# The inverse of the FFT's B stage: six float32r matmuls replaced by plain float32 ones, issued sooner

## The chip, the cores and the metric

The kernel runs on one core of a Trainium2 chip. The time is device microseconds of one execution; the kernel before took 3709.85 us in the median of 3 runs (3709.05 to 3711.37). The profile is of one further execution.

## The reference

Three layers follow each other. The first is a global convolution by FFT over the sequence; the second a feed-forward layer whose activation g is 0 below -1, (h+1)²/4 between -1 and 1 and h above; the third sends each token to the one of eight experts with the largest gate logit.

```python
X = np.fft.rfft(x, axis=1)                        # x: 8 x 3072 x 256, float32
Y = X * (filt_r + 1j * filt_i)[None]
x = np.fft.irfft(Y, n=3072, axis=1).reshape(24576, 256)
x = g(x @ w_in) @ w_out                           # 256 -> 2048 -> 256
out[mask_e] = gate * (np.maximum(x[mask_e] @ w1[e], 0) @ w2[e])   # e = argmax(x @ w_gate), 8 experts, 1024
```

## The kernel before

The FFT of 3072 points is done as 128 x 24, in `fft_unit(u)` for each of the 8 sequences u. Stage A multiplies by a 128x128 table (`a_mm`, 12 half-groups) and stores the result in DRAM scratch. Stage B works on 16 groups g of two blocks each: `b_fwd` (line 459) multiplies by a forward table, `b_mul` and `b_add` (474, 484) multiply by the filter, and `b_inv` (500) multiplies by an inverse table; the result `z` goes back to scratch. `a_inv` (637) then undoes stage A directly into the inputs `xh`, `xl` of the feed-forward layer.

Unit 0 runs first, with plain float32 matmuls. In it the inverse adds two products, of `xq` and of `xs`, in PSUM. Units 1 to 7 run inside the feed-forward layer. They use float32r operands: each is split into a high part (the table's has its last 12 bits cleared) and the rest, and `mm` (356, its matmuls stand as line 361 in the trace) sums three products. For the inverse, ScalarE's `b_yh` (488, instruction at 491) makes the high part `yh` of `xq`, VectorE's `b_yl` (494, instruction at 497) the rest `yl`. The table's two parts come in one load `tt` on GpSimd's queue (`b_tab`, 434).

The feed-forward layer has 48 blocks of 512 tokens, 8 units n each. A unit has four steps: `l1(n, 0)`, `l1(n, 1)`, `l2(n-2, 0)`, `l2(n-2, 1)`, 12 matmuls each (lines 672 and 702). Between them VectorE clamps (679), ScalarE squares (680), VectorE takes a maximum (685), ScalarE rounds to float16 (`gh`, 688) and GpSimd subtracts for the rest (`gl`, 689). The hidden layer's PSUM tile `hps` has two buffers and is freed by line 685.

On TensorE, VectorE, ScalarE and GpSimd the order is the program's, written out by hand: `ev(s, f)` puts f behind step s, and `fire` calls it there. A step number is called a slot when TensorE gets FFT work there. Slots come from a planner (938 to 947): a heap of wishes in order of time, each with a `hold` for the two PSUM buffers `fps` that all FFT matmuls share, and a `bound` below which it may not be put. A group of stage B asks for its forward slot s at `h + b0 + bsp * g`; its table is loaded BT steps before, `b_hi` and `b_lo` (split of the input `a`) 9 and 8 steps before, VectorE's `b_mul` is at s + 2, GpSimd's at s + BX (3), `b_add` at s + BA (4), `b_yh` at s + BH (7 in unit 1, else 8), `b_yl` at s + BLO (9 or 10), and the inverse asks for s + BI (12 or 15). A forward slot's bound keeps it behind the release of buffers by earlier groups.

```python
            for i, (a, b) in enumerate(((ah, bh), (ah, bl), (al, bh))):
                PE.matmul(p, lhsT=a, rhs=b, start=i == 0, stop=i == 2)
```

VectorE and GpSimd also do the routing of each block: small instructions at lines 751 to 801, `hilo` (811) and four scatters by an indirect DMA (815).

Of the kernel before, what the change touches and what calls it, by code (L numbers as in the profile page):

```python
# [29 lines left out]
CVA, WI0 = 4, 8  # L30
AL, AX1, AX2 = 15, 9, 8
BL, BS1, BS2, BM, BV, BZ = 14, 9, 8, 2, 11, 2
BC = ((3, 4, 7, 9, 12, 7), (3, 4, 8, 10, 15, 10))
A1, A2 = (4, 3.5), (-58, 5.0)
B1, B2 = (60, 5.6), (20, 7.9)
ZL, ZB, AI, XL = 20, 8, (17, 12), 2
# [24 lines left out]
def _tables():  # L61
    s1, s2 = np.arange(S1), np.arange(S2)
    a = np.zeros((128, 128))
    ai = np.zeros((128, 128))
    for c in range(64):
        r, i = 2 * c, 2 * c + 1
        if c == 0:
            a[:, r], a[:, i] = 1.0, (-1.0) ** s1
            ai[r], ai[i] = 1.0 / NSEQ, (-1.0) ** s1 / NSEQ
        else:  # L70
            th = 2 * np.pi * ((s1 * c) % S1) / S1
            a[:, r], a[:, i] = np.cos(th), -np.sin(th)
            ai[r], ai[i] = 2 * np.cos(th) / NSEQ, -2 * np.sin(th) / NSEQ
    k2 = np.concatenate([np.arange(12), np.arange(23, 11, -1)])
    bf = np.zeros((NQ, 128, 128))
    bi = np.zeros((NQ, 128, 96))
    fr = np.full((NQ, 128), -1)
    fi = np.full((NQ, 128), -1)
    j12 = np.arange(12)
    for q in range(NQ):  # L80
        for kb in range(2):
            c = 2 * q + kb
            xr = slice(48 * kb, 48 * kb + 24)
            xi = slice(48 * kb + 24, 48 * kb + 48)
            o_r, o_i = 24 * kb, 64 + 24 * kb
            if c > 0:
                th = 2 * np.pi * ((s2[:, None] * (c + 128 * k2[None, :])) % NSEQ) / NSEQ
                co, si = np.cos(th), np.sin(th)
                low = np.arange(24) < 12
                s = np.where(low, -1.0, 1.0)  # L90
                r, i = slice(o_r, o_r + 24), slice(o_i, o_i + 24)
                bf[q, xr, r], bf[q, xi, r] = co, si
                bf[q, xr, i], bf[q, xi, i] = -si * s, co * s
                bi[q, r, xr], bi[q, i, xr] = co.T, (-si * s).T
                bi[q, r, xi], bi[q, i, xi] = si.T, (co * s).T
                f = np.where(low, c + 128 * k2, NSEQ - (c + 128 * k2))
                fr[q, r] = fr[q, i] = fi[q, r] = fi[q, i] = f
            else:
                t0 = 2 * np.pi * ((s2[:, None] * 128 * j12) % NSEQ) / NSEQ
                t1 = 2 * np.pi * ((s2[:, None] * (64 + 128 * j12)) % NSEQ) / NSEQ  # L100
                alt = (-1.0) ** s2
                bf[q, xr, 0:12] = np.cos(t0)
                bf[q, xr, 65:76] = np.sin(t0)[:, 1:]
                bf[q, xr, 64] = alt
                bf[q, xi, 12:24] = np.cos(t1)
                bf[q, xi, 76:88] = np.sin(t1)
                bi[q, 0:12, xr] = (np.where(j12 == 0, 1.0, 2.0) * np.cos(t0)).T
                bi[q, 65:76, xr] = (2 * np.sin(t0)[:, 1:]).T
                bi[q, 64, xr] = alt
                bi[q, 12:24, xi] = (2 * np.cos(t1)).T  # L110
                bi[q, 76:88, xi] = (2 * np.sin(t1)).T
                f = np.concatenate([128 * j12, 64 + 128 * j12])
                fr[q, 0:24] = fi[q, 0:24] = fr[q, 64:88] = fi[q, 64:88] = f
                fr[q, 64] = NSEQ // 2
                fi[q, 0] = fi[q, 64] = -1
    cst = np.zeros((128, C_W))
    cst[:, C_A:C_A + 128] = a
    cst[:, C_AI:C_AI + 128] = ai
    cst[:, C_ID:C_ID + 128] = np.eye(128)
    cst[:, C_TRI:C_TRI + 128] = np.triu(np.ones((128, 128)), 1)  # L120
    cst[:, C_ONE:C_ONE + 128] = 1.0
    cst[:, C_TOK:C_TOK + S2] = 24 * np.arange(128)[:, None] + s2
    cst[:, C_EC:C_EC + E] = np.arange(E) - E
    cst[:, C_ECAP:C_ECAP + E] = np.arange(E) * CAP
    cst[:, C_T:C_T + NT] = np.arange(NT)
    cst[:, C_P] = np.arange(128)
    tab = np.concatenate([bf, bi], axis=2).astype(np.float32)
    hi = (tab.view(np.int32) & ~0xFFF).view(np.float32)
    return cst.astype(np.float32), np.stack([tab, hi, tab - hi]), fr, fi


@with_exitstack
def tile_kernel(ctx, tc, x, w_in, w_out, w_gate, w1, w2, cst, tab, fil, out):
    nc = tc.nc
    V, A, PE, G, SP = nc.vector, nc.scalar, nc.tensor, nc.gpsimd, nc.sync

# [34 lines left out]
    if True:  # L171
# [207 lines left out]
        def fft_unit(u):  # L379
# [44 lines left out]
            def b_load(g):  # L424
                if u:
                    tt = None
                else:
                    tt = alt(u, g, [128, 1, 2, 224], "tt", (qp, "tt"), (fp, "wst"), (qp, "tt"), (fp, "wst"), (fp, "wst"))
                    SP.dma_start(tt, tab[g, :, 0:1])
                tf = more(g, 2, 1, [128, 2, 2 * D], F32, "tf") if u else alt(u, g, [128, 2, 2 * D], "tf", (qp, "tf"), (fp, "xh"), (fp, "xl"))  # L430
                pin(u, g, *((tf, fil[g]) if u or g == 0 else (tf[0:64], fil[g, 0:64])))
                st["b", g] = (tt, tf)

            def b_tab(g):
                tt = more(g, 2, 2, [128, 2, 2, 224], F32R, "tt")
                G.dma_start(tt, tab[g, :, 1:3])
                st["b", g] = (tt,) + st["b", g][1:]

            def b_dup(g):
# [19 lines left out]
            def b_fwd(g):  # L459
                tt, _, t, ag, al = (st["b", g] + (None, None))[0:5]  # L460
                p = ups(u)
                for i in range(2):
                    pi = p[:, i * D:(i + 1) * D]
                    if u:
                        mm(pi, tt[0:96, 0, i, 0:128], tt[0:96, 1, i, 0:128], ag[:, i, :], al[:, i, :])
                    else:
                        mm(pi, tt[0:96, 0, i, 0:128], None, t[:, i, :], None)
                xs = alt(u, g, [128, 2, D], "xs", (qp, "xs"), (fp, "gh"))
                pv = p.rearrange("p (b d) -> p b d", b=2)
                A.activation(xs[0:64], pv[64:128], AF.Copy)  # L470
                A.activation(xs[64:128], pv[0:64], AF.Copy, scale=-1.0)
                st["p", g] = (pv, xs)
# [12 lines left out]
                xq, xs = st["q", g]  # L485
                G.tensor_tensor(xq, xq, xs, op=ALU.add)

            def b_yh(g):
                xq, _ = st["q", g]
                yh = more(g, 2, 1, [128, 2, D], F32R, "yh")  # L490
                A.activation(yh, xq, AF.Copy)
                st["q", g] = (xq, yh)

            def b_yl(g):
                xq, yh = st["q", g]
                yl = more(g, 2, 1, [128, 2, D], F32R, "yl")
                V.tensor_tensor(yl, xq, yh.bitcast(F32), op=ALU.subtract)
                st["q", g] = (yh, yl)

            def b_inv(g):  # L500
                tt = st.pop(("b", g))[0]
                yh, yl = st.pop(("q", g))
                p = ups(u)
                for i in range(2):
                    pi = p[0:96, i * D:(i + 1) * D]
                    if u:
                        mm(pi, tt[:, 0, i, 128:224], tt[:, 1, i, 128:224], yh[:, i], yl[:, i])
                    else:
                        PE.matmul(pi, lhsT=tt[:, 0, i, 128:224], rhs=yh[:, i], start=True, stop=False)
                        PE.matmul(pi, lhsT=tt[:, 0, i, 128:224], rhs=yl[:, i], start=False, stop=True)  # L510
                z = qx[0].tile([96, 2, D], F32, tag="z", name="z", bufs=2) if u else \
                    alt(u, g, [96, 2, D], "z", (qp, "ao"), (qp, "xi"), (qp, "xg"), (qp, "xr"))
                A.activation(z.rearrange("p q d -> p (q d)"), p[0:96], AF.Copy)
# [39 lines left out]
            h = 192 * (u - 1)  # L553
            a0, asp = A1 if u == 1 else A2
            b0, bsp = B1 if u == 1 else B2
            BX, BA, BH, BLO, BI, BT = BC[u > 1]
            ax1, ax2 = (AX1 - 3, AX2 - 3) if u == 1 else (AX1, AX2)

            sa, sb, si = [], [], []
# [6 lines left out]
            def b_bound(g):  # L566
                if len(sb) < g or len(sa) < 2 * NA:
                    return None
                if g == 0:
                    return sa[-1] + BL + 3  # L570
                if g < 3:
                    return sb[0] + 1 + max(BS1, BLO - BM) if g == 2 else 0
                if len(si) < g - 3:
                    return None
                return max(si[g - 4] + BT + 1 if g > 3 else 0, sb[g - 2] + 1 + max(BS1, BLO - BM), sb[g - 3] + 1 + BI + BV - BH)

            def a_slot(s, g, i):
                sa.append(s)
# [6 lines left out]
            def b_slot(s, g):  # L585
# [7 lines left out]
                ev(s + BM, lambda: b_mul(g, 0))  # L593
                ev(s + BX, lambda: b_mul(g, 1))
                ev(s + BA, lambda: b_add(g))
                ev(s + BH, lambda: b_yh(g))
                ev(s + BLO, lambda: b_yl(g))
                slot(s + BI, lambda s: i_slot(s, g), 4 - (u == 1))

            def i_slot(s, g):  # L600
# [581 lines left out]


def _arrays(inputs):
    cst, tab, ir, ii = _tables()

    def lay(a, idx):
        a = np.concatenate([a, np.zeros((1, D), a.dtype)])
# [2 lines left out]
    def pairs(a):  # L1191
# [8 lines left out]
        "w1": a['moe2_w1'],  # L1200
        "w2": a['moe2_w2'],
        "cst": cst,
        "tab": np.ascontiguousarray(tab.reshape(3, NQ // 2, 2, 128, 224).transpose(1, 3, 0, 2, 4)),
        "fil": pairs(np.concatenate([lay(a['filt_r'], ir), lay(a['filt_i'], ii)], axis=2)),
    }

# [13 lines left out]
```

## Time and profile before

| | |
|---|---|
| runs of the kernel before, median (range) | 3709.85 us (3709.05 to 3711.37) |
| the profiled execution | 3699.91 us |
| its span | 3698.1 us |
| TensorE matmuls (PE) busy | 3512.2 us, 95% |
| VectorE (DVE) busy | 2496.0 us, 67% |
| GpSimd (POOL) busy | 1945.8 us, 53% |
| ScalarE (ACT) busy | 1823.4 us, 49% |
| mean granted TensorE clock | 0.983 |

Times are microseconds from the start of the span. A row of a view names a source line (L485 is line 485), an engine, an operation, the tile written and the tiles read, and how often it ran (x112). Matmuls are pipelined: one's duration is longer than the distance to the next one's start, so distances between starts are what a matmul costs TensorE.

### The profile page before, as it was taken

How to read it: one execution, taken by the hardware profiler on the slowest of the kernel's cores; microseconds unless marked ns; L12 is line 12 of the kernel's file. 1: busy time of each engine (PE TensorE's matmuls, PEld its weight loads, DVE VectorE, ACT ScalarE, POOL GpSimd, SP SyncE). 2: the span in 40 equal slices, each digit the busy share in tenths (PEclk: the TensorE clock that was granted, in tenths of full speed). 3: DMA queues.
4: the chain of work that ended last, by engine and by line, in shares of the span. 5: the costliest groups of instructions: out<-in, count | busy, mean ns of one | idle time of the engine just before them, and what ended most of it. 6: DMA issues, size and time to landing. Idle time of an engine off the chain costs nothing. (4 is left out here: it accounts for less than half of the span.)

```text
span 3698.1 us, 75021 instructions
## 1 busy us (share of the span) xinstructions
PE 3512.2 (95%) x30690; PEld 3068.5 (83%) x30690; DVE 2496.0 (67%) x3494; ACT 1823.4 (49%) x2544; POOL 1945.8 (53%) x1428
## 2 busy tenths in 40 slices
PE   6799999999899999999999999999999999999998
PEld 4688888788788878888888888888888888888887
DVE  6678889979888987987888799867632222222222
ACT  4556655655666665666656565554422222222221
POOL 1367666657656765776666576444332222222222
PEclk8899999999999999999999999999999999999999
DMA  9445445434434443444444353101232222222221
GB/s 290 124 132 163 152 142 151 125 124 138 126 122 138 138 129 125 139 128 132 138 127 137 109 145 114 46 24 62 55 84 51 52 52 52 49 53 52 52 52 50
DMA packets 323820, 395.32 MB, mean 107 GB/s; under 512 B 163791, under 2 KB 250063, under 8 KB 322960
## 3 DMA queue, kind: packets, MB, share of 16 engines
q1 hardware_dynamic: 274848, 279.90, 26.6%
q0 software_dynamic: 48624, 110.58, 9.7%
q8 instruction: 243, 3.98, 0.5%
q14 instruction: 105, 0.86, 0.1%
HBM read 439.70 MB, written 120.49 MB: 151 GB/s over the span
## 5 line engine op out<-in xcount | busy, mean ns | idle before, releaser
L689 POOL TENSOR_TENSOR gl<-cl,gh 128x1024 f16<-128x1024 f32 x384 | 821.5, 2139 | 812.6 <-ACT gh L688 527.9
L672 PE MATMUL hps<-xh,wih 128*128 128x256 f16 x3072 | 844.9, 275 | 36.2 <-DVE cl L685 35.7
L672 PE MATMUL hps<-xl,wih 128*128 128x256 f16 x3072 | 842.5, 274 | 1.7 <-DVE xl L646 1.7
L672 PE MATMUL hps<-xh,wil 128*128 128x256 f16 x3072 | 842.2, 274 | 0.0
L702 PE MATMUL yps<-woh,gh 128*128 128x264 f16 x3072 | 721.1, 278 | 13.7 <-ACT ysb L715 13.5
L702 PE MATMUL yps<-wol,gh 128*128 128x264 f16 x3072 | 719.5, 277 | 0.0
L1080 DVE SCALAR_TENSOR_TENSOR hl<-mh,hh 128x1024 f16<-128x1024 f32 x194 | 237.7, 1225 | 686.9 <-ACT hh L1079 678.5
L679 DVE TENSOR_SCALAR cl<-hps,sq 128x1024 f32<-128x1024 f32 x384 | 514.5, 1340 | 273.3 <-PE hps L672 223.5
L680 ACT ACTIVATE cl<-cl,sq 128x1024 f32<-128x1024 f32 x384 | 476.0, 1240 | 448.2 <-DVE cl L679 353.6
L672 PEld LDWEIGHTS <-wih 128*128 128x128 f16 x6144 | 588.0, 98 | 129.8 <-DVE cl L685 37.9
L702 PEld LDWEIGHTS <-gh 128*128 128x128 f16 x6144 | 589.6, 98 | 121.3 <-issue 29.0
L688 ACT ACTIVATE gh<-cl 128x1024 f16<-128x1024 f32 x384 | 406.0, 1057 | 528.7 <-DVE cl L685 527.7
L685 DVE SCALAR_TENSOR_TENSOR cl<-hps,sq,cl 128x1024 f32<-128x1024 f32 x384 | 490.2, 1277 | 101.5 <-ACT cl L680 94.1
L1071 PE MATMUL mh<-xt,wslot 128*128 128x256 f16 x4656 | 540.0, 273 | 0.0
L1079 ACT ACTIVATE hh<-mh 128x1024 f16<-128x1024 f32 x194 | 198.6, 1024 | 620.1 <-PE mh L1071 429.7
L1071 PEld LDWEIGHTS <-wslot 128*128 128x128 f16 x4656 | 455.6, 98 | 52.7
L702 PE MATMUL yps<-woh,gl 128*128 128x264 f16 x3072 | 414.7, 279 | 6.6 <-POOL gl L689 6.6
L1094 PE MATMUL my<-wslot,hh 128*128 128x256 f16 x3104 | 370.8, 273 | 2.8 <-ACT o L1108 2.8
L702 PEld LDWEIGHTS <-gl 128*128 128x128 f16 x3072 | 303.4, 99 | 55.2 <-POOL gl L689 7.2
L1111 POOL DMA_INDIRECT out_dram<-o,me x194 | 191.5, 987 | 281.6 <-issue 200.2
L1094 PEld LDWEIGHTS <-hh 128*128 128x128 f16 x3104 | 303.6, 98 | 38.6 <-issue 3.4
L672 PEld LDWEIGHTS <-wil 128*128 128x128 f16 x3072 | 302.4, 98 | 38.9 <-issue 2.1
(204 smaller groups left out, 4707.5 us busy)
## 6 DMA issues: line engine op xcount, KB each, us to landing
tf<-in_fil_dram SPq DMA_DIRECT2D x113, 512.0 KB
tt<-in_tab_dram POOLq DMA_DIRECT2D x112, 448.0 KB
wst<-in_w_dram SPq DMA_DIRECT2D x128, 256.0 KB
xi<-in_x_dram SPq DMA_DIRECT2D x48, 512.0 KB
scr<-ao SPq DMA_DIRECT2D x48, 512.0 KB
a<-scr SPq DMA_DIRECT2D x128, 192.0 KB
scr<-z SPq DMA_DIRECT2D x128, 192.0 KB
zt<-scr SPq DMA_DIRECT2D x48, 512.0 KB
```

The costliest lines, as they stand in the source:

```text
L672: PE.matmul(p[:, i, :], lhsT=w[:, kt, f * 128:(f + 1) * 128], rhs=xx[:, kt, s], start=a == 0, stop=a == 5)
L679: V.tensor_scalar(cl, p, q[:, 5:6], q[:, 3:4], op0=ALU.max, op1=ALU.min)
L680: A.activation(cl, cl, AF.Square, bias=q[:, 11:12], scale=q[:, 4:5])
L685: V.scalar_tensor_tensor(cl, p, q[:, 7:8], cl, op0=ALU.mult, op1=ALU.max)
L688: A.activation(gh, cl, AF.Copy)
L689: G.tensor_tensor(gl, cl, gh, op=ALU.subtract)
L702: PE.matmul(yps[j][:, 0:WO], lhsT=gg[:, i, j * 128:(j + 1) * 128], rhs=w[:, f, :], start=f == 0 and first, stop=f == NF - 1 and gg is gl)
L1071: PE.matmul(p[:, i, :], lhsT=w[:, wo + kt * FE + f * 128:wo + kt * FE + f * 128 + 128], rhs=xt_[:, xo + kt, :], start=a == 0, stop=a == 5)
L1079: A.activation(hh, p, AF.Relu)
L1080: V.scalar_tensor_tensor(hl, p, 0.0, hh, op0=ALU.max, op1=ALU.subtract)
L1094: PE.matmul(yq[t][j][:, 0:D], lhsT=hx[:, i, j * 128:(j + 1) * 128], rhs=w[:, wo + f * D:wo + (f + 1) * D], start=f == 0 and first, stop=f ...
L1111: G.indirect_dma_start(out=out, out_offset=IOA(ap=me.bitcast(I32)[:, tk, 1:2], axis=0), in_=o, in_offset=None, bounds_check=NTOK - 1, oob_ ...
```

## The change

In units 1 to 7 the inverse multiplies `xq` itself, by the undivided table, with a plain float32 matmul; `b_yh` and `b_yl` are gone. The inverse half of the table is loaded by a second DMA on GpSimd's queue into a tile `ti`, undivided; the forward half keeps its two parts (512 values a partition, then 192, where there were 896). The inverse asks for s + 9 in unit 1 and s + 10 in the others. The bound of a forward slot is written anew: a group's `xq` must not be written before the inverse two groups earlier has read it. Unit 0 keeps its instructions; its table is an array of its own.

```diff
-BC = ((3, 4, 7, 9, 12, 7), (3, 4, 8, 10, 15, 10))
+BC = ((3, 4, 9, 7), (3, 4, 10, 10))
...
-                    SP.dma_start(tt, tab[g, :, 0:1])
+                    SP.dma_start(tt[:, 0], tab[g])
...
             def b_tab(g):
-                tt = more(g, 2, 2, [128, 2, 2, 224], F32R, "tt")
-                G.dma_start(tt, tab[g, :, 1:3])
+                tt = more(g, 2, 2, [128, 512], F32R, "tt"), more(g, 2, 2, [128, 192], F32, "ti")
+                G.dma_start(tt[0], tab2[g, :, 0:512])
+                G.dma_start(tt[1], tab2[g, :, 512:704])
...
-                        mm(pi, tt[0:96, 0, i, 0:128], tt[0:96, 1, i, 0:128], ag[:, i, :], al[:, i, :])
+                        mm(pi, *(tt[0][0:96, o + 128 * i:o + 128 * i + 128] for o in (0, 256)), ag[:, i, :], al[:, i, :])
...
-            def b_yh(g):
-                xq, _ = st["q", g]
-                yh = more(g, 2, 1, [128, 2, D], F32R, "yh")
-                A.activation(yh, xq, AF.Copy)
-                st["q", g] = (xq, yh)
-
-            def b_yl(g):
-                xq, yh = st["q", g]
-                yl = more(g, 2, 1, [128, 2, D], F32R, "yl")
-                V.tensor_tensor(yl, xq, yh.bitcast(F32), op=ALU.subtract)
-                st["q", g] = (yh, yl)
-
             def b_inv(g):
...
                     if u:
-                        mm(pi, tt[:, 0, i, 128:224], tt[:, 1, i, 128:224], yh[:, i], yl[:, i])
+                        mm(pi, tt[1][:, 96 * i:96 * i + 96], None, xq[:, i], None)
...
-            BX, BA, BH, BLO, BI, BT = BC[u > 1]
+            BX, BA, BI, BT = BC[u > 1]
...
-                if g < 3:
-                    return sb[0] + 1 + max(BS1, BLO - BM) if g == 2 else 0
-                if len(si) < g - 3:
+                if len(si) < g - 1:
                     return None
-                return max(si[g - 4] + BT + 1 if g > 3 else 0, sb[g - 2] + 1 + max(BS1, BLO - BM), sb[g - 3] + 1 + BI + BV - BH)
+                return max(si[g - 4] + BT + 1 if g > 3 else 0, sb[g - 2] + 1 + BS1 if g > 1 else 0, si[g - 2] + 1 - BM if g > 1 else 0)
...
-                ev(s + BH, lambda: b_yh(g))
-                ev(s + BLO, lambda: b_yl(g))
```

## Rows read from the trace of the kernel before

**Rows 1.** Busy time (instructions) by stretch: start:end, length, PE, PEld, DVE, ACT, POOL, PEclk, DMA, GB/s.

```profile
135.00:2330.00 2195.00, 2077.95 (x18074) 1805.95 (x18073) 1848.52 (x2449) 1349.14 (x1945) 1465.76 (x1013) 0.99 0.44 133
2330.00:3698.10 1368.10, 1342.09 (x12236) 1196.57 (x12234) 555.45 (x857) 409.34 (x501) 452.57 (x386) 0.99 0.21 52
```

**Rows 2.** Waits of PE, 135 to 2330 us: total us, times, longest us.

```profile
PE hps L672 <- DVE cl L685: 33.2, 22, 3.6
PE fps L361 <- DVE xl L646: 21.8, 11, 4.2
PE yps L702 <- ACT ysb L715: 13.5, 12, 2.1
PE fps L361 <- ACT ao L420: 11.3, 3, 4.1
PE fps L361 <- DVE xq L479: 9.6, 8, 1.7
```

**Rows 3.** Groups by line: shapes, xcount | busy us, mean ns | idle before, by releaser.

```profile
L361 PE MATMUL fps<-yh,tt 128*96 128x256 f32 x448 | 106.9, 301 | 14.7 <-DVE xq L479 8.7 <-DVE xl L646 5.5
...
L361 PE MATMUL fps<-yl,tt 128*96 128x256 f32 x224 | 63.5, 283 | 3.6 <-DVE oh L756 3.6
```

**Rows 4.** Timeline of PE around one inverse: start us, us, instruction.

```profile
1170.18 0.27 PE L672 MATMUL hps<-xh,wil 128*128 128x256 f16 x1
...
1170.99 0.28 PE L672 MATMUL hps<-xh,wih 128*128 128x256 f16 x1
```

**Rows 5.** Timeline of PE in unit 0: two products of an inverse, and the next one.

```profile
68.44 0.59 PE L509 MATMUL hps<-xq,tt 128*96 128x256 f32 x2
...
69.30 0.59 PE L509 MATMUL hps<-xq,tt 128*96 128x256 f32 x2
```

**Rows 6.** Timeline of PE around float32 matmuls of `a_inv`.

```profile
1077.35 0.28 PE L702 MATMUL yps<-wol,gh 128*128 128x264 f16 x1
1077.46 1.05 PE L644 MATMUL fps<-c,zt 128*128 128x128 f32 x8
1078.35 0.28 PE L702 MATMUL yps<-woh,gh 128*128 128x264 f16 x1
```

**Rows 7.** Groups by line, 135 to 2330 us: the two splits of `xq`.

```profile
L497 DVE TENSOR_TENSOR yl<-xq,yh 128x512 fp32r<-128x512 f32 x112 | 163.3, 1458 | 10.3 <-ACT yh L491 10.1
...
L491 ACT ACTIVATE yh<-xq 128x512 fp32r<-128x512 f32 x112 | 69.5, 620 | 27.1 <-POOL xq L486 26.9
```

**Rows 8.** Timeline, 1170 to 1176 us, with [idle before <-releaser].

```profile
1170.51 0.63 ACT L491 ACTIVATE yh<-xq 128x512 fp32r<-128x512 f32 x1 [1.19 <-POOL xq L486]
...
1173.95 0.27 PE L702 MATMUL yps<-woh,gh 128*128 128x264 f16 x1 [1.47 <-ACT ysb L715]
```

**Rows 9.** Groups by line of POOL, 135 to 2330 us.

```profile
L689 POOL TENSOR_TENSOR gl<-cl,gh 128x1024 f16<-128x1024 f32 x326 | 697.9, 2141 | 657.3 <-ACT gh L688 456.8 <-issue 189.5 <-PE fps L361 7.3
...
L436 POOL DMA_DIRECT2D tt<-in_tab_dram x112 | 66.4, 593 | 0.1
```

**Rows 10.** Timeline: a forward, its addition, and the step behind the new slot.

```profile
1152.70 0.36 PE L361 MATMUL fps<-ag,tt 96*128 96x256 f32 x1
...
1167.63 0.28 PE L702 MATMUL yps<-woh,gh 128*128 128x264 f16 x1
...
1169.19 1.28 POOL L486 TENSOR_TENSOR xq<-xq,xs 128x512 f32<-128x512 f32 x1
```

**Rows 11.** Instructions on tile `xq`: ns min/median/max, first and last start us.

```profile
L486 POOL TENSOR_TENSOR xq<-xq,xs x112: 1259/1284/1770, 246.3 to 2314.0; 128x512 f32<-128x512 f32 x112
```

**Rows 12.** Timeline of DVE and POOL, 1156 to 1162 us.

```profile
1156.35 0.68 DVE L479 TENSOR_TENSOR xq<-fps,tf 128x512 f32<-128x512 f32 x1
1156.95 4.72 DVE L811 SCALAR_TENSOR_TENSOR row<-ysb,sm,row 128x256 f16<-128x256 f32 x1
...
1156.58 1.05 POOL L815 DMA_INDIRECT rows<-row,posi  x1 [0.17 <-DVE cl L679]
...
1160.07 1.31 POOL L486 TENSOR_TENSOR xq<-xq,xs 128x512 f32<-128x512 f32 x1
```

More of the change, by code (lines that the diff above doesn't have):

```diff
@@ L128, in _tables, with tile_kernel @@
     hi = (tab.view(np.int32) & ~0xFFF).view(np.float32)
-    return cst.astype(np.float32), np.stack([tab, hi, tab - hi]), fr, fi
+    tab2 = np.stack([hi[:, :, 0:128], (tab - hi)[:, :, 0:128]])
+    return cst.astype(np.float32), tab, tab2, fr, fi
 @with_exitstack
-def tile_kernel(ctx, tc, x, w_in, w_out, w_gate, w1, w2, cst, tab, fil, out):
+def tile_kernel(ctx, tc, x, w_in, w_out, w_gate, w1, w2, cst, tab, tab2, fil, out):
     nc = tc.nc
@@ L486, in b_add @@
                 G.tensor_tensor(xq, xq, xs, op=ALU.add)
-            def b_yh(g):
-                xq, _ = st["q", g]
-                yh = more(g, 2, 1, [128, 2, D], F32R, "yh")
-                A.activation(yh, xq, AF.Copy)
-                st["q", g] = (xq, yh)
-            def b_yl(g):
-                xq, yh = st["q", g]
-                yl = more(g, 2, 1, [128, 2, D], F32R, "yl")
-                V.tensor_tensor(yl, xq, yh.bitcast(F32), op=ALU.subtract)
-                st["q", g] = (yh, yl)
             def b_inv(g):
                 tt = st.pop(("b", g))[0]
-                yh, yl = st.pop(("q", g))
+                xq, xs = st.pop(("q", g))
                 p = ups(u)
@@ L506, in b_inv @@
                     if u:
-                        mm(pi, tt[:, 0, i, 128:224], tt[:, 1, i, 128:224], yh[:, i], yl[:, i])
+                        mm(pi, tt[1][:, 96 * i:96 * i + 96], None, xq[:, i], None)
                     else:
-                        PE.matmul(pi, lhsT=tt[:, 0, i, 128:224], rhs=yh[:, i], start=True, stop=False)
-                        PE.matmul(pi, lhsT=tt[:, 0, i, 128:224], rhs=yl[:, i], start=False, stop=True)
+                        PE.matmul(pi, lhsT=tt[:, 0, i, 128:224], rhs=xq[:, i], start=True, stop=False)
+                        PE.matmul(pi, lhsT=tt[:, 0, i, 128:224], rhs=xs[:, i], start=False, stop=True)
                 z = qx[0].tile([96, 2, D], F32, tag="z", name="z", bufs=2) if u else \
@@ L1184, in _arrays @@
 def _arrays(inputs):
-    cst, tab, ir, ii = _tables()
+    cst, tab, tab2, ir, ii = _tables()
     def lay(a, idx):
@@ L1202, in _arrays @@
         "cst": cst,
-        "tab": np.ascontiguousarray(tab.reshape(3, NQ // 2, 2, 128, 224).transpose(1, 3, 0, 2, 4)),
+        "tab": pairs(tab),
+        "tab2": np.concatenate([tab2.reshape(2, NQ // 2, 2, 128, 128).transpose(1, 3, 0, 2, 4).reshape(NQ // 2, 128, 512),
+                                pairs(tab[:, :, 128:224]).reshape(NQ // 2, 128, 192)], axis=2),
         "fil": pairs(np.concatenate([lay(a['filt_r'], ir), lay(a['filt_i'], ii)], axis=2)),
```

## The prediction, made before the change was run

> **What bounds the kernel now.** I read the stretches first. Of the span of 3698.1 us, 2195 us (135 to 2330 us) are those in which FFT units 1 to 7 run between the steps of the first feed-forward layer, and only there does the change touch anything but a table's layout. In it TensorE is busy 2078 us, VectorE 1849, GpSimd 1466, ScalarE 1349, and the DMA engines 44% of the time; behind 2330 us nothing of the change is left [rows 1]. So TensorE bounds: 2195 - 2078 = 117 us are all that it idles. The second view is who ends that idling. The five longest entries are 33.2 us for `cl` (the half-layer's PSUM tile, freed by VectorE's line 685), 21.8 and 9.6 us for PSUM banks that VectorE frees (lines 646 and 479), 13.5 us for ScalarE's `ysb` and 11.3 us for its `ao`: 89.4 us together, 64.6 of them VectorE's [rows 2]. The reader is to see two prices from this. An instruction added to TensorE costs its whole duration, 112 times. One taken from VectorE or ScalarE is worth only what it shortens of those 117 us.
>
> **The change, part by part.** The sum is made against the profiled execution (3699.91 us), which is 9.94 us under the median of 3709.85; I carry the difference over to the median.
>
> *The inverse on TensorE.* Today a group's inverse is six float32r matmuls of 128x256 (three products, two halves): 448 + 224 instructions over 112 groups [rows 3]. At an undisturbed place the last layer matmul before it starts at 1170.18 and the first one behind it at 1170.99 us; layer matmuls follow each other after 0.11 us, so the inverse costs 0.81 - 0.11 = 0.70 us [rows 4]. The plain form is already here: unit 0 multiplies exactly this shape in float32, and each such matmul is issued as two instructions. Four of them, which is what a group will have, take from 68.44 to 69.30 us, 0.86 us [rows 5]. The other neighbour is the float32 matmul between layer matmuls, eight of 128 columns, as many columns as four of 256: 1078.35 - 1077.35 - 0.11 = 0.89 us [rows 6]. I take 0.86, the same shape: 112 x (0.86 - 0.70) = **+18 us**, all on the path; upper end 112 x 0.19 = 21, and nothing in the rows allows a gain.
> The Trainium skill (FP8 and Floating Point Precision, TensorE Precision Notes) says that a true float32 multiplication is four passes through the array where the reduced one is one, which speaks against the change. By it alone eight passes would replace six, so the 0.70 us would become 0.93, the term 26 us, and the sum -4 instead of -12; no row supports the larger figure, and the measured 0.86 decides.
>
> *What leaves VectorE and ScalarE.* The subtraction `yl` is 163.3 us of VectorE in 112 instructions, 1458 ns in the mean, and the copy `yh` 69.5 us of ScalarE [rows 7]. That is 9% of VectorE's work in the stretch. What of it TensorE sees I take entry by entry from [rows 2].
> For `ysb`: ScalarE runs in order, and at 1170.51 us `yh` has just waited 1.19 us for GpSimd's addition and takes 0.63; the `ysb` behind it then comes late and TensorE waits 1.47 us for it [rows 8]. Without `yh` both go; ten of 13.5 us, since not each of the twelve waits has this cause. For `cl`: one `yl` of 1.46 us ahead of line 685 is as long as one wait in the mean (33.2/22 = 1.5), so between nothing and 33.2 goes; I take 20, because VectorE's queue is often still full of other work. For the banks (21.8 + 9.6) I take a third, 10; for `ao`, whose copy is late for other reasons, nothing. Together **-40 us**; ends: -20 (`ysb` and half of `cl`'s 20) and -67 (`ysb`, `cl`, `xq` whole, half of `xl`).
>
> *The inverse moved sooner.* It is asked for 10 steps behind the forward transform instead of 15 (units 2 to 7), 9 instead of 12 in unit 1. Working the planner's heap through with both sets of constants, I find 10 to 16 steps instead of 15 to 20 in the later units. With it move its ScalarE copy `z`, VectorE's maximum two steps on, and the store on SP's queue, which passes loads of `x`, the filter and the scratch: nothing, the DMA engines being 44% busy [rows 1]; without that cover, the loads behind it would be late by one 192 KB store. The planner also moves forward slots and the routing by up to four steps, which decides where GpSimd's work bunches.
> What the inverse must now wait for is GpSimd's addition directly. A step is 2195/326/4 = 1.68 us, by the 326 `gl` of the stretch [rows 9], ten steps 16.8. In the worked example the forward matmul starts at 1152.70; its addition starts at 1169.19 and ends, after 1.28 us, at 1170.47; yet the step behind which TensorE will now want it is over at 1167.63: 2.84 us late [rows 10]. The same comparison for all 112 additions (246.3 to 2314.0 us, [rows 11]) against their new slots finds 26 late, by 44 us in all. That is the upper end, nothing the lower. Most of the lateness comes from queues that get shorter: in the example VectorE's line 811 lasts 4.72 us while GpSimd runs from 1156.58 through the addition that ends at 1161.38, and it holds `cl`, `gh` and so GpSimd's next work [rows 12]. In units 3 to 7 the forward ahead of it moves four steps off this bunch. I take **+10 us**. Queued behind a waiting inverse is the whole of TensorE, which is why this counts in full.
>
> *The table.* One load becomes two on GpSimd's queue, each with an issue of 0.59 us: +66 us of GpSimd over 112 groups [rows 9], which idles 2195 - 1466 = 729 us. I count nothing; without that cover each addition is 0.6 us later, and that lies inside the 44 us. Fewer bytes go; unit 0's load keeps its bytes.
> *The added wait.* `xq` is now read by TensorE until the inverse, so VectorE's product two groups on must wait for that inverse, and behind it line 679 or 685. The new bound in the planner keeps it at least a step behind; in the example VectorE comes to its product at 1156.35, 3.65 us after the forward's 1152.70 [rows 10, 12]. Nothing.
>
> **Sum:** 18 + 10 - 40 = -12 us: 3688 for the profiled execution, **3698** for the median.
>
> **The rivals.** A difference of 0.2% (7.4 us) is about what a measurement of this kernel can tell from none.
> (a) *Slower: TensorE waits for the addition.* Place: the inverse slot, ten steps behind the forward. For it: the 44 us above, and GpSimd gets 66 us more work. Against: 26 of 112 only, and shorter queues ahead. It decides once the addition ends over 16.8 us behind its forward in about a quarter of the groups, as today. Price 34 of the 44, with 30 of the 40 regained: 18 + 34 - 30 = +22, 3732 us.
> (b) *No difference: the blocking stays.* VectorE's two-input instructions stand still while GpSimd runs back to back; the 4.72 us above belong to a 128x256 instruction of line 811, not to `yl` [rows 12]. If `yl` goes, the next such instruction stands in its place and only its own work is saved. The relief is then 28: 18 + 10 - 28 = 0, 3710 us. The Trainium skill (SBUF — State Buffer, SBUF: two separate sides) has this as an exclusive lock on a shared port pair, under which the loser blocks fully; the trace agrees, with 4.72 us.
> (c) *A larger gain:* relief of 67 and no late addition: 18 - 67 = -49, 3661 us.
> (d) *The change doesn't do what it says:* the slots stay where they were because bounds push them. The planner's arithmetic speaks against; with the inverse late, 18 - 20 = -2, 3708 us.
>
> **How the numbers follow.** Forecast 50%, (a) 23%, (b) 18%, (c) 7%, (d) 2%. Of the forecast's half I put 41 points beyond 0.2% and 9 within, as its terms can miss by 5 either way and more; of (b) 12 points lie within and 3 on each side; (d) within. Faster: 41 + 3 + 7 = 51%; same: 9 + 12 + 2 = 23%; slower: 23 + 3 = 26%. The range reaches from (c) to (a), 3661 to 3732; what is left out are the outer halves of both, under 2 in 10. Cases of both signs have much of it; the forecast's own range is 3680 to 3712.
>
> **What would show it.** In the profile after: four matmuls a group on the inverse's line, some 0.86 us between the layer matmuls on either side; `yl` and `yh` gone and VectorE some 160 us less busy up to 2330 us; two table issues of 0.6 us; TensorE's busy time up by less than 20 us and its waits for `cl` and `ysb` down by 30. The forecast is wrong if a new entry "TensorE waits for GpSimd's `xq`" stands above 25 us (a), or if line 811 and the small routing instructions last as much longer as `yl` was blocked, with `cl`'s 33.2 us still there (b).

## The result, and the profile after

The changed kernel takes 3618.99 us (median of 4 runs, 3611.94 to 3620.06), against 3709.45 us of the kernel before: a ratio of 0.9751 (0.9737 to 0.9765). That is 90 us less where 12 were forecast, and 42 us below the lower end of the range. The direction was right, the size was not.

The profiled executions (3699.91 and 3620.06 us) differ by 80 us, and the stretches say where. This is the view of [rows 1], of the kernel after, its second cut put at the same place in the work:

```profile
135.00:2248.00 2113.00, 2075.95 (x17894) 1794.13 (x17893) 1717.31 (x2343) 1292.18 (x1837) 1521.27 (x1126) 0.99 0.44 133
2248.00:3618.30 1370.30, 1343.73 (x12237) 1196.07 (x12234) 551.42 (x854) 408.42 (x501) 453.14 (x385) 0.99 0.21 52
```

The stretch with the FFT units went from 2195 to 2113 us; behind it nothing changed. TensorE's busy time is the same (2078 before, 2076 after), so its idle time is what fell, from 117 to 37 us. The waits of TensorE, which answer to [rows 2] (the total in us, how many times, the longest in us):

```profile
PE fps L359 <- POOL xq L488: 7.2, 7, 2.0
PE fps L630 <- DVE xl L632: 4.8, 6, 1.2
PE hps L658 <- DVE cl L671: 4.5, 6, 2.3
PE fps L362 <- ACT ao L421: 4.1, 1, 4.1
...
PE yps L688 <- ACT ysb L701: 0.6, 2, 0.3
PE fps L362 <- DVE xq L481: 0.5, 1, 0.5
```

By what ends the wait, the five entries that summed to 89.4 us are 14.5 us now (`xl` now delays line 630, in `a_inv`), and the one large new wait, for GpSimd's addition, costs 7.2 us. (Line numbers have moved: `cl` is freed by line 671, once 685; the routing's 128x256 instruction is line 797, once 811.)

The work itself came out as costed. First one inverse between two layer matmuls, which answers to [rows 4]; then the groups of the inverse, of line 797 and of the two table loads (busy us, mean ns, idle before):

```profile
1176.83 0.27 PE L658 MATMUL hps<-xh,wil 128*128 128x256 f16 x1
1176.94 1.03 PE L359 MATMUL fps<-xq,ti 128*96 128x256 f32 x4
1177.80 0.27 PE L658 MATMUL hps<-xh,wih 128*128 128x256 f16 x1
...
L359 PE MATMUL fps<-xq,ti 128*96 128x256 f32 x448 | 116.2, 382 | 11.6 <-POOL xq L488 7.2 <-issue 2.1 <-DVE winv L853 1.9
...
L797 DVE SCALAR_TENSOR_TENSOR row<-ysb,sm,row 128x256 f16<-128x256 f32 x158 | 133.2, 843 | 0.5
...
L437 POOL DMA_DIRECT2D tt<-in_tab_dram x112 | 65.6, 585 | 0.0
L438 POOL DMA_DIRECT2D ti<-in_tab_dram x112 | 63.8, 569 | 0.0
```

The inverse takes 1177.80 - 1176.83 - 0.11 = 0.86 us. In the median of all 112 places it is 0.865, against 0.715 before by the same measure: +16.8 us. Line 797, which stood still for up to 4.72 us [rows 12], has a mean of 843 ns. Before, this was its row:

```profile
L811 DVE SCALAR_TENSOR_TENSOR row<-ysb,sm,row 128x256 f16<-128x256 f32 x157 | 173.0, 1102 | 1.9 <-ACT row L809 1.8
```

If 16.8 us were added to TensorE and its busy time is the same, something else in it got shorter. Stretches of 5 us show it; the last but two of each row's numbers is the granted clock. Before:

```profile
1025.00:1030.00 5.00, 2.20 (x7) 1.38 (x8) 4.76 (x11) 3.92 (x6) 0.98 (x1) 0.69 0.09 33
1030.00:1035.00 5.00, 5.00 (x30) 3.69 (x29) 4.90 (x9) 3.63 (x6) 4.50 (x3) 0.63 0.00 0
1035.00:1040.00 5.00, 5.00 (x47) 4.54 (x46) 4.97 (x6) 0.70 (x1) 2.82 (x3) 1.00 0.86 263
```

TensorE waits 3.62 us for `ao`, and then the granted clock is down (0.69 and 0.63 in the two stretches, which mix both levels) and 30 instructions fit where 47 do afterwards: a long wait is paid again behind its end. In the stretch with the FFT units, 58.0 us before (135 to 2330 us) and 27.2 us after (135 to 2248 us) were at the half level, 1.2 GHz, and TensorE was busy in 53.9 and 24.0 us of them. Half of the difference in these busy times, 15 us, is an estimate of what TensorE gains by doing that work at 2.4 GHz instead, and it hides the price of the plain matmul in the total.

So 80 us of idle time went, where 40 less 10 were forecast. The experiments ask which part of the change did that.

### The profile page after: what moved, and what is told of

Same layout as the page of the kernel before. It is cut to its first block, busy times and chain, and to the rows that moved or that the text cites. A ratio compares the mean times of both kernels' runs of the same rounds, so it can differ in the third digit from the quotient of the medians.

```text
span 3618.3 us, 74479 instructions
## 1 busy us (share of the span) xinstructions
PE 3510.5 (97%) x30466; PEld 3055.0 (84%) x30466; DVE 2358.1 (65%) x3382; ACT 1762.9 (49%) x2432; POOL 2000.7 (55%) x1540
## 5 line engine op out<-in xcount | busy, mean ns | idle before, releaser
L1042 POOL DMA_INDIRECT wslot<-wsc,widx x97 | 101.7, 1048 | 432.1 <-PE my L1080 427.6
```

## The experiments

Each was timed in three rounds beside the kernel before on the same chip. The kernel before read 3706.11 to 3709.45 us in these rounds, so a difference in us between two versions of different rounds can be some 3 us off; the ratios beside each time are to the kernel before of the same rounds. "Old slots" are the steps of the kernel before (inverse 15 behind the forward in units 2 to 7), "new slots" those of the change (10). Where an expectation names its theories by letters, T holds that the inverse is better the sooner it stands, P that it is PSUM places used again too soon, and G that it is where GpSimd's runs of instructions fall.

**The two halves of the change, each alone.** First the plain inverse in the old slots and with the old bound (`xq` gets a fourth buffer, since it is read for longer):

```diff
-BC = ((3, 4, 9, 7), (3, 4, 10, 10))
+BC = ((3, 4, 7, 9, 12, 7), (3, 4, 8, 10, 15, 10))
```

> Plain float32 inverse without the split, but every slot of the FFT where the kernel before had it (inverse 15 and 12 steps behind the forward, old bounds, xq in four buffers). Theory W (the gain is the work of yl and yh that left VectorE and ScalarE): about 3620 to 3640 us, nearly the whole 90 us, with the waits for cl, ysb and the banks down to a third of the 116 us. Theory S (the gain is the moved slots): about 3700 to 3730 us, no gain or the 18 us of slower matmuls lost.

Measured: 3677.64 us, 0.9912 (0.989 to 0.9934), 31 us faster than before and between the two theories. With 16.8 us of plain matmul in it, the relief is 48 us by the medians; by the profiles, TensorE's idle time fell by 35 us, from 117 to 82. TensorE's waits:

```profile
PE hps L660 <- DVE cl L673: 19.1, 18, 2.4
PE fps L632 <- ACT z L503: 16.8, 7, 3.3
PE fps L362 <- DVE xl L634: 11.3, 6, 4.2
```

`ysb` fell from 13.5 to 4.3 us over the whole stretch (135 to 2311 us) and `cl` by 14, but a wait for `z` came up, and 59 us of the change's gain are missing. Then the other half: the kernel before, split and all, in the new slots and with the new bound, its two split instructions moved along:

```diff
-BC = ((3, 4, 7, 9, 12, 7), (3, 4, 8, 10, 15, 10))
+BC = ((3, 4, 5, 7, 9, 7), (3, 4, 6, 8, 10, 10))
```

> The kernel before with its split kept (yh 6 and yl 8 steps behind the forward, 5 and 7 in unit 1), but with the slots and bounds of the kernel after. Theory W: 3700 us or more, since the work stays, and ScalarE now waits longer for GpSimd's addition. Theory S: about 3610 to 3640 us, even under the kernel after by the 18 us of its slower matmuls.

Measured: 3708.72 us, 1.0005 (0.9995 to 1.0015). That is no gain. The first row is TensorE's largest wait, the second VectorE's wait ahead of `yl`:

```profile
PE fps L361 <- DVE yl L497: 45.5, 30, 3.4
```

```profile
DVE yl L497 <- ACT yh L491: 100.0, 76, 4.3
```

In ten steps the chain addition, `yh`, `yl` doesn't get done, and TensorE stands before the inverse: 45.5 us for `yl`, and 10.7 us more for `yh`. That loss stands against what the moved slots bring, for the wait for `cl`, 33.2 us before, is nearly gone, though `yl` is still there:

```profile
PE hps L670 <- DVE cl L683: 2.8, 2, 2.3
```

The routing's 128x256 instruction shows the same. In the old slots its mean is long even without the split (e1), in the new ones short even with it (e2):

```profile
L799 DVE SCALAR_TENSOR_TENSOR row<-ysb,sm,row 128x256 f16<-128x256 f32 x152 | 186.2, 1225 | 1.9 <-ACT row L797 1.8
```

```profile
L809 DVE SCALAR_TENSOR_TENSOR row<-ysb,sm,row 128x256 f16<-128x256 f32 x152 | 128.3, 844 | 0.6 <-ACT row L807 0.2
```

So one half gives 31 us, the other 0, and both give 90: the parts can't be priced one by one and added, and e2's zero alone is no price of the slots.

**What of `yl` costs so much in the new slots.** The changed kernel gets one instruction per group back, two steps ahead of the inverse, whose result is not used, in four forms that have different parts of `yl`'s cost; the fifth has `yh`'s on ScalarE:

```diff
                 ev(s + BA, lambda: b_add(g))
+                ev(s + BI - 2, lambda: b_du(g))
...
+ e3: V.tensor_tensor(du, xq, xq, op=ALU.subtract)
+ e4: A.activation(du, xq, AF.Copy)
+ e5: V.tensor_reduce(du, xq, axis=AX.X, op=ALU.max)
+ e6: V.tensor_tensor(du, padt, padt, op=ALU.subtract)
+ e7: V.tensor_reduce(du, padt, axis=AX.X, op=ALU.max)
```

The subtraction of `xq`, with two inputs in SBUF and a wait for GpSimd's addition, as `yl` was:

> The kernel after with one added VectorE subtraction of the size and operands of yl (two SBUF inputs) two steps before each inverse, its result unused. Theory W: 30 to 70 us of the gain are given back (3650 to 3690 us). Theory S: under 10 us.

Measured: 3708.62 us, 0.9998 (0.9989 to 1.0008). The whole 90 us are given back by one instruction of VectorE in each group, more than theory W's 70. TensorE idles 99 us in the stretch (135 to 2337 us) where the change idles 37. Its longest wait is for the PSUM bank that `xl` frees, 4.8 us in the change:

```profile
PE fps L636 <- DVE xl L638: 30.7, 21, 2.4
```

The copy on ScalarE:

> The kernel after with one added ScalarE copy of the size of yh two steps before each inverse, its result unused; like yh it has to wait for GpSimd's addition. Theory W: 10 to 30 us are given back (3630 to 3650 us), most of it through ysb. Theory S: under 10 us.

Measured: 3623.79 us, 0.9772 (0.9755 to 0.9788): 5 us, less than expected.

A maximum over `xq`, which has one input and about the same wait:

> As the added subtraction that gave the 90 us back, but a VectorE maximum over the same xq (one SBUF input, the form whose 112 zm never lasted over 0.69 us), so it has the work of 0.68 us and the wait for GpSimd's addition, and no blocking by GpSimd. Theory L (blocking of two-input instructions is what yl cost): 3620 to 3640 us. Theory Q (yl's own time in VectorE's queue, with its wait for the addition): 3680 to 3710 us.

Measured: 3638.89 us, 0.9821 (0.9804 to 0.9837): 20 us.

The subtraction of a constant, which has two inputs and no wait:

> The added subtraction of 128x512, two SBUF inputs, at the same place, but of a constant tile, so it waits for nobody and can only be blocked. Theory L: 3680 to 3710 us, as with xq. Theory Q: 3630 to 3660 us, its 0.68 us alone. Theory D (the wait for the addition in VectorE's queue is what costs): under 3640 us.

Measured: 3671.29 us, 0.9909 (0.9884 to 0.9935): 52 us, in none of the three ranges.

The maximum over the constant, work alone:

> The added maximum over a constant tile: VectorE's work of 0.68 us alone, 112 times, no wait for anybody, no blocking. Theories L and D: 3615 to 3630 us, no difference from the kernel after. Theory Q: 3640 us or more.

Measured: 3633.46 us, 0.9806 (0.979 to 0.9822): 14.5 us, between the ranges. The rows of the added instruction, in the groups of VectorE up to 2250 us (which leaves out the last of the 112 in the slower versions), for e3, e5, e6 and e7 in turn:

```profile
L493 DVE TENSOR_TENSOR du<-xq 128x512 fp32r<-128x512 f32 x105 | 180.1, 1715 | 45.9 <-POOL xq L488 45.9
```

```profile
L493 DVE TENSOR_REDUCE du<-xq 128x1 f32<-128x512 f32 x111 | 75.4, 679 | 51.7 <-POOL xq L488 51.5
```

```profile
L492 DVE TENSOR_TENSOR du<-padt 128x512 fp32r<-128x512 f32 x109 | 153.7, 1410 | 0.0
```

```profile
L492 DVE TENSOR_REDUCE du<-padt 128x2 f32<-128x512 f32 x112 | 75.4, 673 | 0.0
```

Read them against each other. The maxima last 0.68 and 0.67 us and are held by nothing; the subtractions last 1.72 and 1.41 us in the mean, and 0.67 at the least. Work alone costs 14.5 us. The wait, 46 to 52 us of VectorE's time in either, adds 5 (e5 less e7). The subtraction in the maximum's place adds 38 (e6 less e7). The two also differ in what they write, 512 values a partition against one or two. But VectorE's product `xq`, which writes 512 as well and has one input in PSUM and one in SBUF, never lasted over 0.69 us before or in e6, so it is the second SBUF input that the 38 us point to. All of it together is 90, not 58. The form of the instruction is the largest single part; the 32 us or so beyond the sum come only where two inputs and the wait meet, and why was not separated.

**Is sooner better?** The changed kernel with the inverse at other steps (units 2 to 7):

```diff
-BC = ((3, 4, 9, 7), (3, 4, 10, 10))
+BC = ((3, 4, 9, 7), (3, 4, 12, 10))     (e8; 13 in e9, 8 in e10)
```

> The kernel after with the inverse asked for 12 steps behind the forward in units 2 to 7 instead of 10; the planner then puts several forward slots about where they stood before. If sooner is better by itself: halfway, about 3635 to 3655 us. If it is the place of GpSimd's work against VectorE's routing that the slots decide: anything from 3610 to 3680 us, and the mean of line 811's row (843 ns after, 1102 before) goes with the time.

> The kernel after with the inverse asked for 13 steps behind the forward in units 2 to 7. By the planner's plan a PSUM bank is taken again within four steps in 59 places of units 2 to 7 (96 in the kernel before, 77 after, 73 with 12 steps). Theory P (what the slots changed is how soon a bank is taken again): at or under the 3605 us of 12 steps. Theory T (sooner is better by itself): 3640 us or more. Theory G (chance of GpSimd's runs against VectorE's two-input instructions): the time goes with the number of these that last over 3 us (44 with the old slots, 21 after, 16 with 12 steps), not with the banks.

> The same with 8 steps: 77 places within four steps, as after, but 172 within five against 147. GpSimd's addition has two steps less, and should be late more often than the 7 times of the kernel after. Theory T: under 3615 us. Theory P: 3620 to 3635 us. Both with 10 to 40 us of waits for the addition on top, since a step is about 1.6 us.

Measured: 3604.69 us at 12 steps, 0.9723 (0.9707 to 0.9739); 3623.68 at 13, 0.9779 (0.9758 to 0.9801); 3640.21 at 8, 0.9815 (0.9794 to 0.9837); with 3619 at 10 and, from e1 and with its old bound, 3678 at 15. There is a best place and it isn't the soonest, so T falls (between 12 and 10 the intervals just touch). P falls too: by the slots that the planner makes, PSUM places used again within four steps are 77 at 10, 73 at 12 and 59 at 13, and 13 is slower than 12. Nor does the mean of the routing's 128x256 instruction go with the time, as e8's expectation had it: it is 913 ns at 12 steps, more than the 843 at 10, in less time. At 8 steps TensorE's first wait is the one of rival (a):

```profile
PE fps L359 <- POOL xq L488: 32.2, 30, 2.6
```

**GpSimd's part.** The subtraction `al` makes the low part of the forward's input on GpSimd. In e11 it is left out of e1, in e12 out of the changed kernel: the forward multiplies the high part again in its place, so that TensorE's work is the same.

```diff
-                G.tensor_tensor(al, t, ag.bitcast(F32), op=ALU.subtract)
+                st["b", g] = (tt, tf, t, ag, ag)
```

> The plain inverse in the old slots, without GpSimd's 112 subtractions al (the forward multiplies the high part in their place, so the low part of its input is left out, TensorE's work unchanged): GpSimd's runs get shorter by 1.3 us each. Theory G: a good part of the 59 us to the kernel after comes back, 3640 us or less. Theory P: under 15 us, 3662 us or more.

> The kernel after without the same subtractions (the low part of the forward's input left out), as the control: its waits are 37 us in all. Both theories: 3600 to 3620 us, a gain under 20 us.

Measured: 3588.65 us in the old slots, 0.9674 (0.9652 to 0.9697), and 3593.17 us in the new ones, 0.9695 (0.9675 to 0.9716). Without `al` the slots make no difference that counts. With it they make 59 us. The control gains 26 us, more than either theory allowed it. Of the old slots' waits this is left (e11), where e1 had 19.1, 16.8 and 11.3 us:

```profile
PE fps L362 <- ACT ao L421: 5.8, 4, 4.1
PE hps L660 <- DVE cl L673: 3.8, 6, 2.3
```

So what the moved slots bring is freedom from something that `al` does in the old ones: 89 us there (e1 less e11), 26 in the new. Is it GpSimd's time, or its reading? In the old slots again, a fill of an unused tile in `al`'s place takes nearly as much of GpSimd and reads nothing:

```diff
+                G.memset(qx[0].tile([128, 1250], F32, tag="du", name="du", bufs=2), 0.0)
```

> The old slots without al, with GpSimd filling an unused tile of 128x1250 in its place (by the 0.53 us of the 128x520 fill at the start, an estimate of 1.3 us): GpSimd is as busy as with al, but reads nothing from SBUF. The low part of the forward's input is left out as before. If GpSimd's reading instructions block VectorE (theory B): near the 3589 us without al, 3585 to 3610. If it is GpSimd's lateness, that is its time in its own queue (theory Q'): near the 3678 us with al, 3650 or more.

Measured: 3594.58 us, 0.9694 (0.9677 to 0.9712): 6 us above e11, 83 us below e1. The groups of GpSimd, `al` in e1 and the fill in e13:

```profile
L459 POOL TENSOR_TENSOR al<-a,ag 96x512 fp32r<-96x512 f32 x109 | 141.0, 1294 | 9.3 <-ACT ag L454 9.3
```

```profile
L460 POOL MEMSET du<- 128x1250 f32 x112 | 129.9, 1159 | 0.0
```

And the timeline of e13 at the place in the work that [rows 12] show, VectorE and GpSimd:

```profile
1117.31 0.68 DVE L482 TENSOR_TENSOR xq<-fps,tf 128x512 f32<-128x512 f32 x1
1117.90 2.07 DVE L800 SCALAR_TENSOR_TENSOR row<-ysb,sm,row 128x256 f16<-128x256 f32 x1
1119.90 1.27 DVE L674 SCALAR_TENSOR_TENSOR cl<-hps,sq,cl 128x1024 f32<-128x1024 f32 x1
...
1117.33 1.04 POOL L804 DMA_INDIRECT rows<-row,posi  x1 [0.17 <-issue]
1118.38 1.30 POOL L485 TENSOR_TENSOR xs<-xs,tf 128x512 f32<-128x512 f32 x1
1119.60 1.16 POOL L460 MEMSET du<- 128x1250 f32 x1
1120.70 1.29 POOL L489 TENSOR_TENSOR xq<-xq,xs 128x512 f32<-128x512 f32 x1
```

Before, the routing's 128x256 instruction stood from 1156.95 to 1161.67, through the whole run of GpSimd. Between the two instructions that [rows 12] show, that run was

```profile
1157.62 1.32 POOL L482 TENSOR_TENSOR xs<-xs,tf 128x512 f32<-128x512 f32 x1
1158.84 1.32 POOL L457 TENSOR_TENSOR al<-a,ag 96x512 fp32r<-96x512 f32 x1
```

Here the routing's instruction starts the same way, and it ends at 1119.97, as the product `xs` (to 1119.68) gives way to the fill; `cl` follows at once. The Trainium skill (SBUF — State Buffer, SBUF: two separate sides) describes this: an exclusive lock between a VectorE instruction with two SBUF inputs and a GpSimd instruction that reads SBUF. The trace agrees for the fill, which reads nothing (2.07 us where it had been 4.72), and for the maxima of e5 and e7, which have one input (0.68 and 0.67 us). One input alone doesn't keep every instruction free, though: the routing's 128x4 tensor_scalar on `sm` (line 767) took between 0.16 and 3.49 us before.

e11 to e13 compute other values than the change, so their routing can differ. But the last layer runs the same number of matmuls, and the time went from the stretch of the FFT units: the last addition of `xq` starts at 2294 us in e1, at 2199 in e11 and at 2207 in e13.

Not fully separated: the fill is 10% shorter than `al`, doesn't wait for `ag` (9.3 us in e1), and the forward doesn't wait for it (in e1 no wait of TensorE's names `al`). A fill in the new slots was not run. Nor did a count of long VectorE instructions over the whole kernel order all the versions as their times do; e9 is slower than the change with no more of them. How the lost time spreads from the blocked instruction to each wait stays open, beyond the wait for `xl` in e3.

**A version to keep.** The inverse at 12 steps, and the forward in plain float32 as well, so that `al`, `ag` and the second table load go:

```diff
-                        mm(pi, *(tt[0][0:96, o + 128 * i:o + 128 * i + 128] for o in (0, 256)), ag[:, i, :], al[:, i, :])
+                        mm(pi, tt[0:96, 224 * i:224 * i + 128], None, t[:, i, :], None)
...
-                ev(s - BS1, lambda: b_hi(g))
-                ev(s - BS2, lambda: b_lo(g))
```

> A version meant to be kept: with 12 steps for the inverse, the forward transform too multiplies plain float32, so al, ag and their table's split go (112 subtractions of GpSimd, 112 copies of ScalarE, one load instead of two a group). TensorE gets 112 x 0.15 = 16 us more; the control without al gained 26 us at 10 steps, and 30 us of waits are left at 12. Expected 3590 to 3610 us, against 3605 us for 12 steps alone; over 3615 if what is left of the waits has other causes.

Measured: 3600.96 us, 0.9711 (0.9694 to 0.9729), within the range expected and 18 us faster than the change (15 by the ratios). Its stretch:

```profile
135.00:2230.00 2095.00, 2078.95 (x17659) 1790.15 (x17659) 1570.70 (x2345) 1234.97 (x1725) 1314.57 (x902) 1.00 0.40 127
```

TensorE idles 16 us of 2095 here, and e8, with its split forward, 31 (busy 2064.19); but the plain forward keeps TensorE busier, and the two differ by less than their intervals. There is little idle time left to win in this stretch, so a larger gain would have to come from TensorE's own work.

## Why the prediction was wrong

Point by point, by its own terms:

- *The inverse on TensorE, +18.* Right: 16.8, from 0.86 us at each of 112 places, as unit 0 showed [rows 5].
- *What leaves VectorE and ScalarE, -40.* Right in size where it can be measured alone: in the old slots (e1) 48 by the medians, 35 by the idle time. `ysb` gave 9 of its 13.5 where 10 were taken, and `cl` 14 where 20 were. The new wait for `z`, 16.8 us, stood in no term; e2 has it too (16.7), so it doesn't belong to the old slots alone.
- *The table, 0.* Consistent: the two loads take 129 us of GpSimd where one took 66 [rows 9], and its waits for the addition are 7.2 us. This wasn't tried alone.
- *The wait for the addition, +10.* Close: 7.2 us in 7 waits. Rival (a) needed a quarter of the groups; at 8 steps 30 of 112 wait for 32 us, so its mechanism is real, two steps further.
- *The added wait on `xq`, 0.* It held: among VectorE's waits after, none of the product's (line 481) is ended by the inverse (line 359).
- *The inverse moved sooner.* This is the step that failed. It said that the planner also moves forward slots and the routing, "which decides where GpSimd's work bunches", and then put only the +10 of lateness into the sum. The moved slots bring 59 us on top of e1's 31, where the sum had 10 us lost. I had the row that shows the mechanism [rows 12], and used it for the rival in which blocking stays and for lateness, never as a gain. e11 to e13 tie the 59 us to GpSimd's `al` in the old slots: without it, or with a fill in its place, the old slots cost next to nothing (3589 and 3595 us, against 3593 in the new ones without it).
- *The form of the sum.* Adding terms was itself wrong. The slots without the removal give 0 (e2, where 56 us of waits for the late split stand against the relief), the removal without the slots 31 (e1), both 90. So the plain inverse is worth 90 in the new slots (e2 to the change) and 31 in the old ones, and in the new ones an instruction like `yl` alone undoes everything (e3).
- *The clock.* No term stood for it. By the estimate above, 15 us of the gain come from work of TensorE's that no longer runs at half clock behind long waits. The upper bound of rival (c), 67 us of relief, was too low for that reason as well as for the slots.

Rival (b) fell: the next two-input instruction did not take `yl`'s place. Line 811's mean went from 1102 to 843 ns, and `cl`'s wait from 33.2 to 4.5 us. But its mechanism, the blocking, is what the slots change, and in e1 the same routing instruction still has a mean of 1225 ns. Rival (d) fell: the slots moved.

## What to carry to other kernels

Price an instruction on VectorE by the form it has and by what runs on GpSimd beside it, not by its own work: the same place in the queue cost 14.5 us for a maximum with one SBUF input and 52 for a subtraction with two. Where a change both removes an instruction and moves slots, predict the four combinations, not two terms; an added instruction in each form (with its wait or without, two inputs or one) prices what was removed in one run each. After taking work out, try the slots again on both sides, since the best place moves: 12 steps beat 13 and 8 here, and 10 by little.

## What the runs showed of the hardware

At the place in [rows 12] a VectorE instruction with two SBUF inputs is held across a whole run of GpSimd instructions, not for the one beside it: 4.72 us over four of them before, and 2.07 us in e13, where the run is broken by a fill. A plain float32 matmul of 128x256 is issued as two instructions and takes 0.43 us (0.865 for two of them), a float32r one 0.119 (0.715 for six), so that two plain ones replace six for 0.15 us more. And around the end of a wait of 3.62 us TensorE's granted clock fell to the half level and stayed there for 6.8 us; in the stretch with the FFT units TensorE was busy at that level for 53.9 us before and 24.0 after.
